# Four-block tiles for the sliding-window scores, the maxima's low part on GpSimd, packed constants and new tables of orders in a four-layer attention kernel

## The chip, the cores and the metric

The kernel runs on one core of one Trainium2 chip. The metric is the device time of one execution in microseconds (us). Engines are named as the profile names them: PE is TensorE (PEld its weight loads), DVE is VectorE, ACT is ScalarE, POOL is GpSimd, SP is SyncE, which issues the DMAs. Each engine works through its own list of instructions in order, and semaphores tie the lists together.

## The reference

Four layers, each added to its input: A, B, A, B, over 2048 positions of width 512 with 32 heads of 16. A attends to 8 keys at distances 0, 2, ... 14. B attends to the last 256 keys, its own among them. Layer A and layer B have one set of weights each, used twice.

```python
x = x + _A_ref(_layernorm(x), A_wqkv, A_wo)
x = x + _B_ref(_layernorm(x), B_wqkv, B_wo)     # and both again
# inside B
scores = jnp.einsum("bhqd,bhkd->bhqk", q, k) * (Dh ** -0.5)
mask = (idx[:, None] - idx[None, :] >= 0) & (idx[:, None] - idx[None, :] < 256)
p = _softmax(jnp.where(mask, scores, -1e9), axis=-1)
o = jnp.einsum("bhqk,bhkd->bhqd", p, v)
```

## The kernel before, in words

The positions are cut into 8 chunks of 256 queries. The unit of work is one chunk of one layer: 16 pairs, first A on chunk n, then B on chunk n (`A0`, `B0`, ... `A15`, `B15`; the second pair of layers begins at `A8`). Projections keep float32 accuracy with float16 operands: each operand is a high and a low half, and a product is three matmuls (lines 802 to 804 and 821 to 823).

**Layer B.** A chunk of 256 queries is two query blocks of 128. Each query block needs three key blocks of 128: a far one cut by a triangle (call it L), a middle one that is needed whole (F), and its own, cut by the other triangle (H). The stacked queries and keys lie in `stk`; two heads share a matmul pass, one in rows 0 to 63 and one in rows 64 to 127 of PE ("par"). Score tiles are PSUM tiles `q_sc` of 128 x 2 x 512 float32 (two banks); there are two of them for all of what follows.

- *Maxima first.* The 32 heads go in four groups `j`. For each of the 8 pairs (u, query block) in a group, PE writes a tile `sq` of two heads x three key blocks (lines 1129 and 1132), DVE merges the two triangles into one block with COPY_PREDICATED (line 1148, two heads x 128 elements) and takes the maximum with TENSOR_REDUCE (line 1150, 512 elements). In the first chunk of a layer, where L does not exist, line 1143 does both for one head at a time.
- *The maxima's way.* DVE transposes the group's 32 maxima (`mturn`, line 1158), ACT makes their high half in float16 (`mhigh`, line 1161), DVE the low half (`mlow`, line 1164, scalar_tensor_tensor on `mr` and `mt`, both in SBUF). SP writes them to DRAM (`md`, line 1169) and back into two rows of `stk` (line 1174), so that the second score pass subtracts the maximum inside the matmul.
- *Probabilities.* For each of a group's two head-quads `hq`, key chunk b (the one before, or this one) and half i, PE writes a transposed score tile `sk` of three blocks (lines 1203 and 1205), ACT takes the exponential into `p` (line 1209, 768 elements), and after two of these POOL zeroes the triangles (line 1218, 1024 elements). Then `values` (line 1235) multiplies with the values `vt` in float32: 8 matmuls, four of 256 columns and four of 128, in four column groups of PE.

**Layer A** multiplies keys and queries elementwise (`pr`, line 950, added at 957), reduces with `sel` on PE (964), spreads the softmax's weights with `selt` (1023), and weighs the values (`pw`, 1036; summed at 1041 on DVE or 1043 to 1045 on POOL).

**Weights** are prepared by `prep` at the start: squares on ACT (674), a transpose on PE (681, tiles `pam`), a scale from DVE (687 to 693), sent to all partitions by PE (696) and copied (700); then the high half on ACT (724) and the low half on DVE (726).

**What sets the order.** Every step is entered by `plan.add(engine, cost, function, reads, writes)`. The table `ORDER` gives each step its place on its engine's list, part by part (`pA`, `pB`, `W`, `A0`, `B0`, ...); a negative entry sends a step that may run on either of two engines to the other one. `Plan.order` then lays the steps of all engines out in one sequence. `W` holds `IDLE` steps of three matmuls on `selt` that only keep PE's clock up while the weights load.

Of the kernel before, what the change touches and what calls it, by code (L numbers as in the profile page):

```python
# [1386 lines left out]
```

## Time and profile before

| | |
|---|---|
| three runs | 1388.22, 1389.94, 1395.54 us (median 1389.94) |
| the profiled execution | 1386.94 us, of which the span from first to last instruction is 1385.2 us |
| mean granted PE clock | 0.988 |
| ACT | busy 736.3 us (53%) in 1075 instructions |
| DMA | 139.29 MB, 101 GB/s in the mean |
| idle steps before the work starts | 110 steps of three matmuls |

"Busy" is time in which an engine had at least one instruction under way; matmul ends are modelled, so a busy PE isn't a full PE. In a group of instructions stand the line, the engine, the operation, what it writes and reads, the shapes, the count, the busy time and the mean of one in ns. A wait is written "who line <- whom line: us in total, times, longest". A row of the timeline has its start, its duration and the merged count at the end.

### The profile page before, as it was taken

What the parts mean: (1) busy time and instruction counts of PE and PEld (TensorE: products, weight loads), DVE (VectorE), ACT (ScalarE), POOL (GpSimd) and SP (SyncE); (2) the same over time, 40 slices, a digit from 0 to 9 for tenths busy, and PEclk for the clock granted to TensorE, in tenths of its full rate; (3) what the DMA queues carried; (4) which work ended last, traced back from release to release, by engine and by line L of the source; (5) the groups of instructions that cost most, each with busy time, mean ns of one, the idle gap of its engine ahead of it and who ended that gap; (6) DMA issues with size and microseconds to landing.
All of it is one profiled execution on the core that took longest, in us unless ns stands there. A gap on an engine that the chain in (4) does not pass through costs nothing.

```text
span 1385.2 us, 34153 instructions
## 1 busy us (share of the span) xinstructions
PE 1278.8 (92%) x13546; PEld 743.3 (54%) x13546; DVE 1183.7 (85%) x2030; ACT 736.3 (53%) x1075; POOL 946.4 (68%) x963
## 2 busy tenths in 40 slices
PE   7888999999999999998899979999999999998976
PEld 6655645555555555555455545655565555543532
DVE  4898898898988898797898979988988989888674
ACT  6442535655555564564555445565655565555554
POOL 3285778786776657968576647869688877866342
PEclk9999999999999999999999999999999999999989
DMA  7425144434334452333434334444434335234312
GB/s 217 119 51 138 36 116 105 114 91 113 84 97 109 100 130 75 91 94 85 121 78 122 100 96 86 119 113 103 123 90 120 85 95 119 49 108 109 113 47 62
DMA packets 172416, 139.29 MB, mean 101 GB/s; under 512 B 105184, under 2 KB 131296, under 8 KB 172256
## 3 DMA queue, kind: packets, MB, share of 16 engines
q1 hardware_dynamic: 172000, 136.85, 37.9%
q8 instruction: 106, 1.74, 0.5%
q14 instruction: 54, 0.44, 0.1%
q10 hardware_dynamic: 256, 0.26, 0.1%
HBM read 67.11 MB, written 43.48 MB: 80 GB/s over the span
## 4 chain that ended last, share of the span: by engine, by line
PE 37%; DVE 33%; DMA 8%; issue 7%; POOL 6%; ACT 5%; SPq 4%; DVEq 0%; POOLq 0%; ACTq 0%
DVE m L1150 8%; PE av L1235 6%; DVE sq L1148 5%; PE pq L802 5%; DVE pw L1036 4%; PE pq L803 4%; PE pq L804 4%; PE sk L1203 3%; PE sq L1129 2%; ACT p L1209 2%; DVE pr L950 2%; DVE j L1143 2%; PE po L821 2%; DVE mt L1164 2%; PE po L823 2%
## 5 line engine op out<-in xcount | busy, mean ns | idle before, releaser
L1209 ACT ACTIVATE p<-sk,sclB 128x768 f32<-128x768 f32 x480 | 423.6, 900 | 274.5 <-PE sk L1205 252.6
L1218 POOL TENSOR_SCALAR_AFFINE_SELECT p<-p 128x1024 f32<-128x1024 f32 x240 | 266.1, 1117 | 171.0 <-ACT p L1209 167.3
L1150 DVE TENSOR_REDUCE m<-sq 128x2 f32<-128x512 f32 x448 | 310.4, 693 | 15.4
L1148 DVE COPY_PREDICATED sq<-maskt,sq 128x256 f32<-128x256 int16 x448 | 188.9, 422 | 77.0 <-PE sq L1132 70.2
L1235 PE MATMUL av<-p,v 128*32 128x128 f32 (+1 forms) x3840 | 200.2, 334 | 7.3 <-DVE el L1067 4.0
L950 POOL TENSOR_TENSOR pr<-kv,q 128x1024 f32<-128x1024 f32 x69 | 155.1, 2256 | 21.5 <-DVE pr L957 13.1
L1203 PE MATMUL sk<-stk,stk 64*128 64x256 f16 x960 | 130.6, 279 | 26.1 <-DVE m L1150 16.6
L1235 PEld LDWEIGHTS av<-p,v 128*32 128x32 f32 x3840 | 104.2, 110 | 94.0 <-issue 36.3
L1036 DVE TENSOR_TENSOR pw<-pb,kv 128x1024 f32<-128x1024 f32 x128 | 152.1, 1213 | 1.6 <-PE pb L1023 1.4
L1043 POOL TENSOR_TENSOR pw<-pw 128x512 f32<-128x512 f32 x92 | 117.1, 1273 | 51.6 <-DVE pw L1036 51.5
L1129 PE MATMUL sq<-stk,stk 48*128 48x128 f16 (+1 forms) x896 | 112.8, 252 | 22.6 <-DVE m L1150 13.3
L1132 PE MATMUL sq<-stk,stk 48*128 48x128 f16 (+1 forms) x1024 | 124.2, 246 | 7.9 <-DVE m L1143 5.6
L1203 PEld LDWEIGHTS <-stk 64*128 64x128 f16 x960 | 52.4, 93 | 129.1 <-issue 69.4
L1129 PEld LDWEIGHTS <-stk 48*128 48x128 f16 x896 | 48.1, 93 | 114.5 <-issue 58.1
L957 POOL TENSOR_TENSOR pr<-pr,pr 128x1024 f32<-128x1024 f32 x35 | 83.8, 2396 | 32.7 <-DVE pr L950 32.3
L1205 PE MATMUL sk<-stk,stk 64*128 64x128 f16 x960 | 104.5, 217 | 0.0
L950 DVE TENSOR_TENSOR pr<-kv,q 128x1024 f32<-128x1024 f32 x59 | 86.4, 1478 | 3.1 <-POOL pr L957 3.0
L802 PE MATMUL pq<-xh,wA1h 128*128 128x256 f16 x256 | 70.7, 276 | 3.6 <-DMA xh<-xm 3.2
L1064 ACT ACTIVATE eh<-pq 128x512 f16<-128x512 f32 x64 | 37.3, 596 | 67.7 <-PE pq L804 49.0
L803 PE MATMUL pq<-xl,wA1h 128*128 128x256 f16 x256 | 70.2, 274 | 3.1 <-DMA xl<-xn 3.1
L802 PE MATMUL pq<-xh,wB1h 128*128 128x256 f16 x256 | 70.2, 274 | 2.4 <-DVE xr L859 1.3
L1044 POOL TENSOR_TENSOR pw<-pw 128x256 f32<-128x256 f32 x92 | 67.0, 728 | 7.2
(184 smaller groups left out, 3185.3 us busy)
## 6 DMA issues: line engine op xcount, KB each, us to landing
stk<-re SPq DMA_DIRECT2D x256, 96.0 KB
re<-eh SPq DMA_DIRECT2D x128, 128.0 KB
xm<-xr SPq DMA_DIRECT2D x32, 256.0 KB
re<-el SPq DMA_DIRECT2D x64, 128.0 KB
xr<-xm SPq DMA_DIRECT2D x16, 512.0 KB
oc<-os SPq DMA_DIRECT2D x120, 64.0 KB
os<-scr SPq DMA_DIRECT2D x15, 512.0 KB
x<-in_A_x_dram SPq DMA_DIRECT2D x8, 512.0 KB
```

The costliest lines, as they stand in the source:

```text
L802: nc.tensor.matmul(ps[mp].t[:, i], wh, xh, start=k == 0, stop=False)
L803: nc.tensor.matmul(ps[mp].t[:, i], wh, xl, start=False, stop=False)
L950: E.tensor_mul(pr.t, window(kv[1].t, m, P * n, P), qb)
L1036: nc.vector.tensor_mul(pw.t, pb.t.unsqueeze(1).broadcast_to([P, 2, W, 64]), v)
L1129: nc.tensor.matmul(ps.t[:, par, 0 : (2 - qb) * P], lhs, stk[hf, bef][r, col, qb * P :], start=True, stop=True)
L1132: nc.tensor.matmul(ps.t[:, par, (2 - qb) * P : 3 * P], lhs, stk[hf, now][r, col, : (1 + qb) * P], start=True, stop=True)
L1148: nc.vector.copy_predicated(t[:, :, 0:P], maskt[:, 0:P].bitcast(I16).unsqueeze(1).broadcast_to([P, 2, P]), t[:, :, 2 * P : 3 * P])
L1150: nc.vector.tensor_reduce(out=m[:, 0:2, u, qb], in_=t[:, :, 0 : 2 * P], op=ALU.max, axis=AX.X)
L1203: nc.tensor.matmul(o[:, two], k[:, jf * P : (jf + 1) * P], q, start=True, stop=True)
L1209: nc.scalar.activation(pt.t[:, :, 2 * i : 2 * i + 2].rearrange("p s m q -> p m s q"), ps.t[:, :, : 3 * P].rearrange("p m (s q) -> p m s q" ...
L1218: nc.gpsimd.affine_select(out=v, in_=v, pattern=[[0, 8], [-1 if b == 0 else 1, P]], compare_op=ALU.is_gt if b == 0 else ALU.is_ge, fill=0. ...
L1235: nc.tensor.matmul(o, v[:, jj, 17 * h : 17 * h + 32], rhs, start=z == 0 and (b == 0 or first), stop=z == 1 and b == 1, tile_position=(0, 3 ...
```

## The change

Names of the new kernel are used with its own line numbers, which the lists below show.

1. **Maxima by kind of block.** The tiles now hold four blocks per head instead of three. A group has four tiles `st` (both triangles of both query blocks of one u: 2 heads x 4 blocks) and two tiles `sf` (the whole blocks F of two u's). Every matmul has 128 columns. `m` has two halves, one for each kind, joined by a new maximum on DVE ahead of the transpose (two operands in SBUF).
2. **Probabilities by kind of block.** For each head-quad there are three tiles of kinds F, L and H, eight matmuls of 128 columns each, an exponential of 1024 elements, a mask on POOL for L and H alone, and `values` of 8 matmuls of 128 columns. `p` has 5 buffers of 1080 elements instead of 3 of 1536.
3. **The maxima's low half** is taken on POOL, from maxima that ACT has scaled first (two ACT instructions instead of one).
4. **B's weights** are scaled in place on ACT, copied to float16 on ACT, and subtracted by a step that may run on DVE or POOL.
5. **Packed constants.** The identity lies in the third value buffer until `border(2)` overwrites it; the scales lie in two tiles; `maskt` has 256 columns instead of 384; some small tiles have one buffer instead of two.
6. **New tables.** All of `ORDER` is new, and `IDLE` is 80 instead of 110. Of the steps that may run on two engines, DVE now has 66 of the products `pr` (59 before) and 18 of the scalings `oc` (7), POOL 62 (69) and 12 (23); the others moved by one or two.

```diff
-IDLE = 110
+IDLE = 80
-                       ("pxt", 2), ("pp6", 3), ("pe2", 1), ...
+                       ("pxt", 2), ("pp6", 5), ("pe2", 1), ...
+                if T == "B":
+                    plan.add("ACT", 1.05, lambda j=j, s=s, at=at: nc.scalar.activation(at(j), at(j), AF.Copy, scale=psc[T, s][:, 1:2]),
+                             r=[*touched[j], vsc[s]], w=touched[j])
...
+                    plan.add("POOL", 2.2, lambda E, f=split: f("l", E), r=[...], w=[vwt[T, s]], mode="S", alt=("DVE", 1.13))
...
+            def block(ps, at, u, qb, back, hf=hf, hp=hp):
+                col = 4 * hp + u
+                kt, kb = (bef if qb == 0 else now, 1 - qb) if back is None else (bef if back else now, qb)
+                for par in range(2):
+                    r = slice(64 * par, 64 * par + 48)
+                    nc.tensor.matmul(ps.t[:, par, at * P : (at + 1) * P], stk[hf, 0][r, col, qb * P : (qb + 1) * P],
+                                     stk[hf, kt][r, col, kb * P : (kb + 1) * P], start=True, stop=True)
...
+                            nc.vector.copy_predicated(v[:, :, 0::2], maskt[:, 0:P]..., v[:, :, 1::2])
+                            nc.vector.tensor_reduce(out=m[:, 0, :, us[0]], in_=v[:, :, 0::2], op=ALU.max, axis=AX.X)
...
+                    nc.vector.tensor_reduce(out=o, in_=v, op=ALU.max, axis=AX.X)
...
             def mturn(m=m, mr=mr):
-                nc.vector.transpose(mr.t, m.rearrange("p a u q -> p (a u q)"))
+                a, b = (m[:, z, :, :, 1] if first else m[:, z].rearrange("p a u q -> p (a u q)") for z in range(2))
+                nc.vector.tensor_tensor(out=a, in0=a, in1=b, op=ALU.max)
+                nc.vector.transpose(mr.t, m.rearrange("p z a u q -> p (z a u q)"))
             def mhigh(mr=mr, mt=mt):
-                nc.scalar.activation(mt.t[:, 0], mr.t, AF.Copy, scale=1.0 / MC)
+                nc.scalar.activation(mr.t, mr.t, AF.Copy, scale=1.0 / MC)
+                nc.scalar.copy(mt.t[:, 0], mr.t)
             def mlow(mr=mr, mt=mt):
-                nc.vector.scalar_tensor_tensor(mt.t[:, 1], mr.t, 1.0 / MC, mt.t[:, 0], op0=ALU.mult, op1=ALU.subtract)
+                nc.gpsimd.tensor_tensor(out=mt.t[:, 1], in0=mr.t, in1=mt.t[:, 0], op=ALU.subtract)
...
-                for b in ((1,) if first else (0, 1)):
-                    for i in range(2):
+                for kind in "FH" if first else "FLH":
+                    pt = buf("pp6", [P, 4, HALO + C], F32, "p6", ...)
...
+                        nc.scalar.activation(o, i, AF.Exp, scale=scl["B", 1])
+                    if kind != "F":
...
+                                nc.tensor.matmul(acc.t[32 * mm : 32 * mm + 32, hq, qb * P : (qb + 1) * P], v[:, 17 * (H * kb + h) : ...],
+                                                 p[:, mm % 2, 2 * (mm // 2) + qb], ..., tile_position=(0, 32 * mm), skip_group_check=True)
...
+    plan.add("POOL", 0.4, lambda: border(2), w=[vidf, vborder])
```

What this and the tables make of the lists is shown at three places.

DVE, the end of group 0 of chunk 7 in the first layer B, before: `sq_7_0_u_qb` are the group's tiles, `m_123` its maxima, `pw` belongs to layer A.

```order
L1148 COPY_PREDICATED sq_7_0_2_1_9774<-maskt,sq_7_0_2_1_9774 128x2x128
L1150 TENSOR_REDUCE m_123<-sq_7_0_2_1_9774 128x2
L1148 COPY_PREDICATED sq_7_0_3_0_9788<-maskt,sq_7_0_3_0_9788 128x2x128
L1150 TENSOR_REDUCE m_123<-sq_7_0_3_0_9788 128x2
L1036 TENSOR_TENSOR pw_0_0_1_9821<-pb_0_0_1_9795,kv_0_2_9234 128x1024
L1036 TENSOR_TENSOR pw_0_0_0_9843<-pb_0_0_0_9793,kv_0_2_9234 128x1024
L1148 COPY_PREDICATED sq_7_0_0_1_9838<-maskt,sq_7_0_0_1_9838 128x2x128
L1150 TENSOR_REDUCE m_123<-sq_7_0_0_1_9838 128x2
L1148 COPY_PREDICATED sq_7_0_3_1_9863<-maskt,sq_7_0_3_1_9863 128x2x128
L1150 TENSOR_REDUCE m_123<-sq_7_0_3_1_9863 128x2
L1158 STREAM_TRANSPOSE mr_7_0_9891<-m_123 128x32
L1036 TENSOR_TENSOR pw_0_1_0_9898<-pb_0_1_0_9869,kv_0_2_9234 128x1024
```

The same place now: `st_7_0_u` are tiles of triangles, `sf_7_0_w` tiles of whole blocks, `m_118` the maxima.

```order
L1142 COPY_PREDICATED st_7_0_1_10547<-maskt,st_7_0_1_10547 128x4x128
L1143 TENSOR_REDUCE m_118<-st_7_0_1_10547 128x2x2
L1142 COPY_PREDICATED st_7_0_2_10566<-maskt,st_7_0_2_10566 128x4x128
L1143 TENSOR_REDUCE m_118<-st_7_0_2_10566 128x2x2
L1162 TENSOR_REDUCE m_118<-sf_7_0_0_10586 128x2x4
L1162 TENSOR_REDUCE m_118<-sf_7_0_1_10612 128x2x4
L1035 TENSOR_TENSOR pw_0_0_0_10634<-pb_0_0_0_10624,kv_0_2_10052 128x1024
L1142 COPY_PREDICATED st_7_0_3_10650<-maskt,st_7_0_3_10650 128x4x128
L1143 TENSOR_REDUCE m_118<-st_7_0_3_10650 128x2x2
L1035 TENSOR_TENSOR pw_0_0_1_10688<-pb_0_0_1_10626,kv_0_2_10052 128x1024
L1172 TENSOR_TENSOR m_118<-m_118 128x16
L1173 STREAM_TRANSPOSE mr_7_0_10718<-m_118 128x32
```

A group's maxima were 16 instructions over eight tiles and are now 10 over six; the joining maximum (L1172) stands ahead of the transpose, and the low half no longer follows it on DVE.

POOL at the same place, before: it sums layer A's `pw` in three steps each, and zeroes triangles of `p`.

```order
L1043 TENSOR_TENSOR pw_0_0_0_9843<-pw_0_0_0_9843 128x2x256
L1044 TENSOR_TENSOR pw_0_0_0_9843<-pw_0_0_0_9843 128x2x128
L1045 TENSOR_TENSOR o_0_9845<-pw_0_0_0_9843 128x2x64
L1218 AFFINE_SELECT p_6_6_0_9819<-p_6_6_0_9819 128x1024
L935 COPY ha_0_2_9944<-kv_0_2_9234 128x56
```

And now, with the low half (`mt`) between two such sums:

```order
L1043 TENSOR_TENSOR pw_0_0_1_10688<-pw_0_0_1_10688 128x2x128
L1044 TENSOR_TENSOR o_0_10666<-pw_0_0_1_10688 128x2x64
L1180 TENSOR_TENSOR mt_7_0_10772<-mr_7_0_10718,mt_7_0_10772 128x32
L1042 TENSOR_TENSOR pw_0_1_1_10746<-pw_0_1_1_10746 128x2x256
L1043 TENSOR_TENSOR pw_0_1_1_10746<-pw_0_1_1_10746 128x2x128
```

POOL has 64 such low halves; if the maxima are late, the sum of `pw_0_1_1` and what follows waits behind this one.

PE at the start, before: the first transpose of squares (`pam`) is the 152nd row of its list.

```order
L1347 LDWEIGHTS selt
L1347 MATMUL idle_323<-selt 128x256
L681 MATMUL pamA_327<-idf,amA_254 1x128
L1347 LDWEIGHTS selt
L1347 MATMUL idle_331<-selt 128x256
```

Now it is the 20th:

```order
L1365 LDWEIGHTS selt
L1365 MATMUL idle_192<-selt 128x256
L669 MATMUL pamA_219<-v_124,amA_209 1x128
L1365 LDWEIGHTS selt
L1365 MATMUL idle_223<-selt 128x256
```

25 idle steps (75 matmuls) stood ahead of it, now 3 (9 matmuls). Counted over PE's whole list, the form of the matmul (whole array, two row halves, four column groups) changes 1227 times before and 1003 times now, and the columns that stream through in each form are the same but for the idle steps.

More of the change, by code (lines that the diff above doesn't have):

```diff
@@ L623 @@
     wt, vwt, psc, scl, vscl = {}, {}, {}, {}, {}
+    scales = [cst.tile([P, 10], F32, name=f"scales{i}") for i in range(2)]
     for T in "AB":
         for s in range(4):
-            psc[T, s] = cst.tile([P, 2], F32, name=f"psc{T}{s}")
+            psc[T, s] = scales["AB".index(T)][:, 2 * s : 2 * s + 2]
             for z in "hl":
@@ L742, in norm @@
         rs = buf("psm", [P, 2, 2], F32, "rs", f"rs{l}_{c}")
-        b6 = buf("psm", [P, 2, 6], F32, "b6", f"b6{l}_{c}")
+        b6 = [buf("ps1", [P, 6], F32, "b6", f"b6{l}_{c}_{t}") for t in range(2)]
         vmv, vrs = [Val(mv), Val(mv)], Val(rs)
@@ new lines, in layer_b, with tri, tritop, full @@
+            vq = [vst[hf, 0, hp], vst[hf, now, hp], *([] if first else [vst[hf, bef, hp]])]
+            for w in range(2):
+                for us in ((2 * w, 2 * w + 1),) if first else ((2 * w,), (2 * w + 1,)):
+                    ps = buf("q_sc", [P, 2, 512], F32, "sc", f"st{l}_{c}_{j}_{us[0]}")
+                    vps = Val(ps)
+                    def tri(us=us, ps=ps, block=block):
+                        at = 0
+                        for u in us:
+                            for qb in range(2):
+                                for back in (False,) if first else (True, False):
+                                    block(ps, at, u, qb, back)
+                                    at += 1
+                    def tritop(us=us, ps=ps, m=m):
+                        v = ps.t.rearrange("p a (x k) -> p a x k", k=P)
+                        if first:
+                            nc.vector.tensor_tensor(out=v, in0=v, in1=maskt[:, P:].unsqueeze(1).unsqueeze(1).broadcast_to([P, 2, 4, P]), op=ALU.add)
+                            nc.vector.tensor_reduce(out=m[:, 0, :, us[0] : us[0] + 2].rearrange("p a u q -> p a (u q)"), in_=v, op=ALU.max, axis=AX.X)
+                        else:
+                            nc.vector.copy_predicated(v[:, :, 0::2], maskt[:, 0:P].bitcast(I16).unsqueeze(1).unsqueeze(1).broadcast_to([P, 2, 2, P]), v[:, :, 1::2])
+                            nc.vector.tensor_reduce(out=m[:, 0, :, us[0]], in_=v[:, :, 0::2], op=ALU.max, axis=AX.X)
+                    plan.add("PE", 0.235, tri, r=vq, w=[vps], mode="R", act=0.2)
+                    plan.add("DVE", 2.4 if first else 1.33, tritop, r=[vps], w=[vm])
+                if first and w == 0:
+                    continue
+                ps = buf("q_sc", [P, 2, 512], F32, "sc", f"sf{l}_{c}_{j}_{w}")
+                vps = Val(ps)
+                def full(w=w, ps=ps, block=block):
+                    for at in range(4):
+                        if first:
+                            block(ps, at, at, 1, None)
+                        else:
+                            block(ps, at, 2 * w + at // 2, at % 2, None)
+                def fulltop(w=w, ps=ps, m=m):
+                    v = ps.t.rearrange("p a (x k) -> p a x k", k=P)
+                    o = m[:, 1, :, :, 1] if first else m[:, 1, :, 2 * w : 2 * w + 2].rearrange("p a u q -> p a (u q)")
+                    nc.vector.tensor_reduce(out=o, in_=v, op=ALU.max, axis=AX.X)
+                plan.add("PE", 0.235, full, r=vq, w=[vps], mode="R", act=0.2)
+                plan.add("DVE", 1.2, fulltop, r=[vps], w=[vm])
@@ L1225, in values @@
-                    def values(hh=hh, hq=hq, b=b, pt=pt, jf=jf, jo=jo, qo=qo, two=two, one_=one_, acc=acc):
-                        v = vt[(c - 1 + b) % 3]
-                        for z in range(2):
-                            jj = jf if z == 0 else jo
+                                    nc.tensor.matmul(ps.t[:, par, at * P : (at + 1) * P], stk[hf, kt][r, col, kb * P : (kb + 1) * P],
+                                                     stk[hf, 0][r, col, qb * P : (qb + 1) * P], start=True, stop=True)
@@ new lines, in layer_b, with mask @@
+                    used = [now] if first else used
+                    plan.add("PE", 0.235 if len(qbs) == 2 else 0.125, scores, r=[vst[hf, 0, hp], vst[hf, "m", hp], *(vst[hf, x, hp] for x in used)],
+                             w=[vps], mode="R", act=0.2 if len(qbs) == 2 else 0.1)
+                    plan.add("ACT", 1.06 if len(qbs) == 2 else 0.6, expo, r=[vps, vscl["B", 1]], w=[vp])
+                    if kind != "F":
+                        def mask(kind=kind, view=view):
+                            v = view().rearrange("p a x k -> p (a x) k")
+                            nc.gpsimd.affine_select(out=v, in_=v, pattern=[[0, 8], [-1 if kind == "L" else 1, P]],
+                                                    compare_op=ALU.is_gt if kind == "L" else ALU.is_ge, fill=0.0, base=0,
+                                                    channel_multiplier=1 if kind == "L" else -1)
+                        v0, vp = vp, Val(pt)
+                        plan.add("POOL", 1.06, mask, r=[v0], w=[vp], mode="S")
@@ L1238, in layer_b @@
                     nxt = Val(acc)
-                    plan.add("PE", 0.67, values, r=[vp2, *vvt[(c - 1 + b) % 3], *([chain] if chain else [])], w=[vacc, nxt], mode="C", act=0.16)
+                    bs = {"F": (0, 1), "L": (0,), "H": (1,)}[kind]
+                    bs = (1,) if first else bs
+                    plan.add("PE", 0.45 if len(qbs) == 2 else 0.23, values, r=[vp, *(x for b in bs for x in vvt[(c - 1 + b) % 3]), *([chain] if chain else [])],
+                             w=[vacc, nxt], mode="C", act=0.107 if len(qbs) == 2 else 0.055)
```

173 lines of the change are left out of this document (73 added, 100 removed), and 477 rows, old and new, of the table ORDER.

## The prediction

> **What bounds the kernel now.** I read the page's busy shares first, then the windows, then the chain of work that ended last, then the waits. The page:
>
> ```profile
> span 1385.2 us, 34153 instructions
> PE 1278.8 (92%) x13546; PEld 743.3 (54%) x13546; DVE 1183.7 (85%) x2030; ACT 736.3 (53%) x1075; POOL 946.4 (68%) x963
> PE 37%; DVE 33%; DMA 8%; issue 7%; POOL 6%; ACT 5%; SPq 4%; DVEq 0%; POOLq 0%; ACTq 0%
> DVE m L1150 8%; PE av L1235 6%; DVE sq L1148 5%; PE pq L802 5%; DVE pw L1036 4%; PE pq L803 4%; PE pq L804 4%; PE sk L1203 3%; PE sq L1129 2%; ACT p L1209 2%; DVE pr L950 2%; DVE j L1143 2%; PE po L821 2%; DVE mt L1164 2%; PE po L823 2%
> ```
>
> Two windows of the steady stage (length, then busy time of PE, PEld, DVE, ACT, POOL), and three waits:
>
> ```profile
> 880.00:960.00 80.00, 78.73 (x896) 45.34 (x898) 72.52 (x116) 46.37 (x68) 63.71 (x64) 1.00 0.39 104
> 1040.00:1120.00 80.00, 77.97 (x865) 45.58 (x864) 69.77 (x110) 46.15 (x68) 64.80 (x64) 1.00 0.41 107
> DVE sq L1148 <- PE sq L1132: 70.2, 98, 3.3
> PE sk L1203 <- DVE m L1150: 16.6, 29, 1.8
> PE sq L1129 <- DVE m L1150: 13.3, 29, 1.3
> ```
>
> PE and DVE bound the steady stage together. Both are nearly full (DVE 87 to 91% of a window), the chain passes back and forth between them, and each waits for the other at the two score tiles in PSUM. ACT (53%) and POOL (68%) have room. So DVE's work counts with a weight between its rows' share of the chain and one, and the same holds for PE.
>
> **Maxima on DVE.** The old tile costs, by shape and by start times:
>
> ```profile
> L1150 DVE TENSOR_REDUCE m<-sq 128x2 f32<-128x512 f32 x448 | 310.4, 693 | 15.4
> L1148 DVE COPY_PREDICATED sq<-maskt,sq 128x256 f32<-128x256 int16 x448 | 188.9, 422 | 77.0 <-PE sq L1132 70.2 <-ACT p L1209 3.3 <-PE sq L1129 1.1
> 710.04 0.42 DVE L1148 COPY_PREDICATED sq<-maskt,sq 128x256 f32<-128x256 int16 x1
> 710.49 0.69 DVE L1150 TENSOR_REDUCE m<-sq 128x2 f32<-128x512 f32 x1
> 711.10 0.42 DVE L1148 COPY_PREDICATED sq<-maskt,sq 128x256 f32<-128x256 int16 x1
> L1036 DVE TENSOR_TENSOR pw<-pb,kv 128x1024 f32<-128x1024 f32 x128 | 152.1, 1213 | 1.6 <-PE pb L1023 1.4
> L1143 DVE CUSTOM_DVE_ANT_0 j<-sq,maskt 128x256 bf16<-128x256 f32 x64 | 27.0, 421 | 4.3 <-PE sq L1132 1.4 <-DVE m L1143 0.5
> L1143 DVE CUSTOM_DVE_ANT_0 j<-sq,maskt 128x128 bf16<-128x128 f32 x64 | 18.6, 290 | 10.4 <-PE sq L1132 7.6
> ```
>
> Copy to reduce is 0.45 us, reduce to next copy 0.61: 1.06 a tile, 8.48 a group. L1143 gains 131 ns for 128 elements, so 256 more cost some 0.26 us, 512 more 0.52. A triangle tile is then 0.45 + 0.26 + 0.61 = 1.32, a whole one 0.61 + 0.52 = 1.13 (the 1024 elements of L1036 took 1.21), a group 4 x 1.32 + 2 x 1.13 = 7.54. That is 0.94 less; with 1.21 for the whole tiles 0.78 less. I take 0.86, times 56 groups = -48 us of DVE. In the first chunks (8 groups) three larger instructions replace L1143's; nothing is taken. On the chain L1150 has 8% of 1385 = 111 us of its 310, L1148 5% = 69 of 189, so weight 0.37; at weight one it is -48. I take 0.6, because the windows leave DVE only about a tenth idle: **-29** (-18 to -48).
>
> **The low half and the joining maximum.** Lines of `mt`, and the operation that POOL holds longest:
>
> ```profile
> L1164 DVE SCALAR_TENSOR_TENSOR mt<-mr,mt x64: 156/408/2339, 134.2 to 1352.6; 128x32 f16<-128x32 f32 x64
> L1164 DVE SCALAR_TENSOR_TENSOR mt<-mr,mt 128x32 f16<-128x32 f32 x64 | 39.9, 623 | 4.7 <-ACT mt L1161 4.4
> L950 POOL TENSOR_TENSOR pr<-kv,q 128x1024 f32<-128x1024 f32 x69 | 155.1, 2256 | 21.5 <-DVE pr L957 13.1 <-ACT kv L928 7.0 <-ACT q L926 1.0
> L950 DVE TENSOR_TENSOR pr<-kv,q 128x1024 f32<-128x1024 f32 x59 | 86.4, 1478 | 3.1 <-POOL pr L957 3.0
> L1045 POOL TENSOR_TENSOR o<-pw 128x128 f32<-128x128 f32 x92 | 43.1, 469 | 7.2
> PE sk L1203 <- DMA stk<-md: 2.3, 3, 1.1
> PEld L1203 <- DMA stk<-md: 0.9, 1, 0.9
> ```
>
> 32 elements need 156 ns, and took up to 2339, about POOL's 2256: a DVE operation with two operands in SBUF stands still while POOL works on its own. Removing it gives DVE 39.9 us back. The joining maximum is again such an operation, 64 times, on 16 elements: 156 ns each if it never met POOL (10 us), 623 if it meets it as often (39.9). I take the second, since nothing in the lists keeps it away from POOL: **0** (at best -30 on DVE, -18 in time).
>
> The Trainium skill states the rule (SBUF — State Buffer, "Who interferes with whom"): a VectorE instruction with two SBUF inputs contends with a GpSimd instruction that reads SBUF, and whichever starts first holds the shared ports to its end. It speaks against the change, since what is taken from DVE comes back as another two-input instruction; the row's 156 to 2339 ns agrees, and by the rule the sum is my 0.
>
> On POOL the low half costs at most 64 x 0.469 = 30 us, covered by its idle third. Its queue is new: an instruction that waits there for ACT holds up the masks behind it, and the maxima come later by ACT's second step and by what stands ahead on POOL. PE has waited 3.2 us in all for these DMAs, so there was slack: 0.
>
> **PE.** The score matmuls are cut from 256 to 128 columns.
>
> ```profile
> 717.22 1.51 PE L1235 MATMUL av<-p,v 128*32 128x256 f32 x32
> 718.66 0.28 PE L1203 MATMUL sk<-stk,stk 64*128 64x256 f16 x2
> 718.78 0.22 PE L1205 MATMUL sk<-stk,stk 64*128 64x128 f16 x2
> 718.93 0.28 PE L802 MATMUL pq<-xh,wA0h 128*128 128x256 f16 x1
> 726.05 0.28 PE L1129 MATMUL sq<-stk,stk 48*128 48x256 f16 x2
> 726.17 0.22 PE L1132 MATMUL sq<-stk,stk 48*128 48x128 f16 x2
> 726.22 0.28 PE L1203 MATMUL sk<-stk,stk 64*128 64x256 f16 x2
> 726.34 0.22 PE L1205 MATMUL sk<-stk,stk 64*128 64x128 f16 x2
> ```
>
> By start times a pair of 256 columns takes 0.12 us and a pair of 128 takes 0.05, each with its own weights, so a tile goes from 0.17 to 4 x 0.055 = 0.22 and a group from 16 x 0.17 = 2.7 to 12 x 0.22 = 2.6. The values (1.44 us for two steps of 16 records) stream the same columns. Nothing, then, in the rate. But where the form changes (718.78 to 718.93) 0.15 passes instead of 0.05: some 0.09 lost, and the list has 224 fewer changes. 224 x 0.09 = -20 us of PE; at PE's share of the chain (37% of 1385 = 512 of 1279 busy, 0.40) -8, at weight one -20. I take **-9**. Fewer tiles also mean a quarter fewer hand-overs; PE's own waits for DVE's maxima were 16.6 + 13.3 = 30 us: **-5** (0 to -7).
>
> **Exponentials and moved steps.**
>
> ```profile
> L1209 ACT ACTIVATE p<-sk,sclB 128x768 f32<-128x768 f32 x480 | 423.6, 900 | 274.5 <-PE sk L1205 252.6 <-PE av L1235 10.1 <-POOL pw L1044 4.3
> L1309 DVE TENSOR_TENSOR oc<-oc,os 128x512 f32<-128x512 f32 x7 | 5.6, 814 | 1.7 <-DMA stk<-re 1.1 <-issue 0.6
> ```
>
> 480 exponentials become 352 of 1024 elements and 16 of 512. In proportion one takes 1.2 us (422 + 10 = 432 us); with a fixed part it is less. About even, on an engine that waited 252.6 us for PE here: 0. DVE takes over 7 products (7 x 1.478) and 11 scalings (11 x 0.814), some +19, less five steps of other kinds that went to POOL, by the same two rows 4 to 7: +14, at 0.37 **+5** (0 to +14).
>
> **The start.**
>
> ```profile
> 7.43 11.11 PE L1347 MATMUL idle<-selt 128*128 128x256 f16 x75 [7.43 <-POOL selt L619]
> 8.45 0.19 ACT L674 ACTIVATION_READ_ACCUMULATOR wA1l<-stk 128x1 f32 x1
> 24.08 2.47 DVE L726 SCALAR_TENSOR_TENSOR wA1l<-stk,pscA,wA1h 128x1024 f16<-128x1024 f32 x2
> 26.80 0.27 PE L802 MATMUL pq<-xh,wA1h 128*128 128x256 f16 x1
> 92.90 5.13 DVE L726 SCALAR_TENSOR_TENSOR wB1l<-stk,pscB,wB1h 128x512 f16<-128x512 f32 x2
> ```
>
> The squares of the first weights were ready at 8.64, but 75 idle matmuls held PE until 18.5; nine of them take 1.3 us. That could bring the first projection, at 26.80, forward by up to 9.7. The old run's next gate was `wA1l`, done at 26.5; its ACT step now waits while ACT normalises x and squares the second weights, so I take -6. B's low halves were slow on DVE (5.13 us for one half of `wB1l`); as plain subtractions some go to POOL, but ACT gets eight scalings more: -2. Together **-8** (0 to -14).
>
> **Sum.** -29 + 0 - 9 - 5 + 5 - 8 = -46 us. From the profiled execution's 1386.94 (span 1385.2 and 1.7 around it) that is 1341; the median of the three runs, 1389.94, lies 3 above the profiled one, so the forecast for a median is **1344 us**, and by the bounds of the terms some 1303 to 1377.
>
> **Rivals.**
> - *PE alone sets the pace.* It has 92% against 85%, and 97 to 98% in the windows. DVE's 48 us are then worth only idle time; left are -20 and -8: 1362. Against it: PE's ends are modelled, and DVE has 33% of the chain.
> - *The port takes it back.* DVE has 18 more two-input steps and the maximum; if each maximum meets a whole product of POOL (2.26 us) instead of 0.62, that is 64 x 1.64 = 105 us on DVE, at 0.37 +39: 1383. For it: the maximum of 2339; against: the median of 408.
> - *The port stays free for the maximum.* -18: 1326.
> - *Slower: the maxima arrive late.* PE takes its list in order, so if a `sk` tile stands at its head while the low half waits on POOL, everything on PE waits. ACT's second step is 0.2 us, half a product on POOL 1.1: 64 x 1.3 = 83 us if all of it shows, 1427. It turns the sign when more than 46 / 64 = 0.7 us a group shows. Against it: the 3.2 us of waits for `stk<-md`.
> - *Slower: short matmuls are bound by their weights.* If a pair of 128 columns can't follow a pair of 128 at 0.055 us but takes 0.10 us, near a weight load's time, when four stand in a row, a tile loses 4 x 0.04 = 0.16, 728 tiles 116 us of PE, at 0.40 to 1 +46 to +116: about 1425. At weight 0.40 it turns the sign from 0.04 a pair on. Against it: 726.17 to 726.22, though no run of four stands in this trace.
>
> The Trainium skill has a rule for that (TensorE: Matmul & The Clock Gate, "Back-to-back issue gap"): a stream of weight load and matmul pairs of 128 columns goes at about 81 ns for each matmul, not the 55 of the columns. By it eight matmuls would take 0.65 us a tile and the kernel would be far slower; the pair at 726.17 passed in 0.05 us, so the trace doesn't agree for two row halves.
>
> That the lists don't hold what the change says is out: DVE's 896 instructions for maxima beyond the first chunks are 560 in the new list.
>
> **How the numbers follow.** Forecast 0.58, PE alone 0.14, port worse 0.08, port free 0.08, late maxima 0.07, short matmuls 0.05. From no change a measurement here can tell about 0.5%, 7 us. Faster: 0.56 + 0.13 + 0.04 + 0.08 = 0.81; same: 0.02 + 0.01 + 0.03 + 0.01 = 0.07; slower: the rest, 0.12. The range 1303 to 1383 takes in the forecast's bounds, PE alone, port free and half of port worse, and leaves out some 0.16.
>
> **What would show it.** In the new profile COPY_PREDICATED of 512 near 0.69 us, the reduction of 1024 near 1.2; the joining maximum with a mean near 0.6; DVE's busy time down by some 50 to 60, PE's waits for tiles down; the first projection near 21 us; waits for `stk<-md` still a few us. Wrong would be: DVE less busy but the span the same (PE), score pairs of 128 that start over 0.08 apart, or `sk` waiting for `md`.

## The result and the profile after

The changed kernel takes 1368.6 us in the median of 4 runs (1366.8 to 1370.5), the kernel before beside it 1389.8 (1388.2 to 1395.5): a ratio of 0.984 with a 95% interval of 0.981 to 0.987. It is faster by 21 us; the forecast was 46 us faster, 1344 us in a range of 1303 to 1383. The profiled execution took 1367.4 us, with a span of 1365.6.

The page of the changed kernel, span, busy times and the chain's shares by engine:

```profile
span 1365.6 us, 40923 instructions
PE 1247.1 (91%) x17296; PEld 825.0 (60%) x17296; DVE 1149.1 (84%) x1489; ACT 732.7 (54%) x1035; POOL 945.8 (69%) x1018
PE 35%; DVE 28%; DMA 11%; POOL 10%; issue 6%; SPq 5%; ACT 5%; DVEq 0%; POOLq 0%; ACTq 0%
```

VectorE has 34.6 us less to do than before and TensorE 31.7. The chain holds less of both and more DMA (8 to 11%) and GpSimd (6 to 10%). Two windows of the steady stage, at the places shown of before, say that nothing else has become the bound there:

```profile
880.00:960.00 80.00, 77.15 (x1157) 52.26 (x1159) 72.12 (x95) 44.37 (x63) 67.14 (x71) 1.00 0.40 102
1040.00:1120.00 80.00, 78.45 (x1180) 53.39 (x1175) 71.09 (x96) 48.82 (x67) 60.35 (x68) 1.00 0.42 109
```

TensorE and VectorE are as full as before. The new instructions on VectorE, from the page's groups and, for the last row, from the list of one tile's operations (minimum, median and maximum in ns):

```profile
L1142 DVE COPY_PREDICATED st<-maskt,st 128x512 f32<-128x512 int16 x224 | 154.0, 687 | 48.5 <-PE st L1119 40.1
L1143 DVE TENSOR_REDUCE m<-st 128x4 f32<-128x512 f32 x224 | 154.9, 691 | 7.7
L1162 DVE TENSOR_REDUCE m<-sf 128x8 f32<-128x1024 f32 x120 | 145.3, 1215 | 25.3 <-PE sf L1119 24.8
L1172 DVE TENSOR_TENSOR m<-m x64: 111/264/1935, 144.4 to 1331.1; 128x16 f32<-128x16 f32 x56, 128x8 f32<-128x8 f32 x8
```

The prices are those of the prediction (0.69 and 1.2 us; the joining maximum has a mean of 0.48 where 0.62 was taken). VectorE's idle time ahead of these instructions is nearly what it was: 77.0 us before L1148, now 48.5 and 25.3 us. So the steady stage looks as forecast, and the start doesn't. Windows of the start, of the kernel before and of the changed one:

```profile
80.00:90.00 10.00, 9.31 (x65) 6.26 (x66) 8.52 (x29) 5.55 (x8) 9.17 (x9) 1.00 0.24 72
150.00:160.00 10.00, 9.21 (x96) 6.30 (x95) 7.88 (x36) 5.43 (x8) 5.57 (x8) 1.00 0.22 42
```

```profile
80.00:90.00 10.00, 0.00 (x0) 0.00 (x0) 8.73 (x13) 4.90 (x7) 0.16 (x1) 0.50 0.25 52
90.00:100.00 10.00, 8.44 (x35) 4.15 (x36) 2.12 (x4) 0.00 (x0) 5.55 (x8) 0.69 0.01 2
150.00:160.00 10.00, 3.97 (x16) 1.46 (x17) 5.84 (x5) 1.10 (x2) 5.70 (x3) 0.71 0.14 32
```

From 80 to 90 us TensorE does nothing at all, and it is granted half its clock. Who is waited for there is in the timeline and the waits of the changed kernel:

```profile
79.97 8.00 SPq L1354 DMA_DIRECT2D stk<-pad  x8
89.84 1.67 POOL L852 TENSOR_TENSOR ol<-o,oh 128x512 f16<-128x512 f32 x1 [17.58 <-DMA stk<-pad]
91.56 0.61 PE L822 MATMUL po<-wA3h,ol 128*128 128x512 f16 x1 [14.73 <-POOL ol L852]
```

```profile
POOL ol L852 <- DMA stk<-pad: 25.0, 2, 17.6
PE po L822 <- POOL ol L852: 21.9, 4, 14.7
```

GpSimd wants to make the low half of A's output (`ol`) at 72 us and stands still for 17.6 us, until transfers that read `pad` have landed; a second such wait, 7.5 us, ends at 154. `pad` holds the constant rows that stand below the keys and queries. In the changed kernel it takes turns with A's output halves in their two rotating buffers, and its transfers write over the place where B's weights are staged, so they can't start before these have been split. In the kernel before it had a buffer of its own.

To see where time is won and lost, I take from each trace the end of the fourth copy of `av` in a chunk (the evictions of B's accumulated values, L1270 before, L1287 now). The difference to the kernel before, in us, with the two main experiments beside it:

| end of | before | changed | e1_pad_own | e5_pad_early |
|---|---|---|---|---|
| chunk 0 | 204 | +15 | +4 | -1 |
| chunk 3 | 449 | +17 | +6 | -1 |
| chunk 7 | 782 | 0 | -14 | -15 |
| chunk 11 | 1093 | -3 | -18 | -19 |
| chunk 14 | 1320 | -13 | -29 | -32 |
| span | 1385.2 | -19.6 | -32.6 | -38.9 |

The changed kernel is 15 us late after its first chunk, wins 28 in the next fourteen and 6 in the last stretch.

### The profile page after: what moved, and what is told of

It is laid out like the page before. It is cut to its first block, busy times and chain, and to the rows that moved or that the text cites. A ratio compares the mean times of both kernels' runs of the same rounds, so it can differ in the third digit from the quotient of the medians.

```text
span 1365.6 us, 40923 instructions
## 1 busy us (share of the span) xinstructions
PE 1247.1 (91%) x17296; PEld 825.0 (60%) x17296; DVE 1149.1 (84%) x1489; ACT 732.7 (54%) x1035; POOL 945.8 (69%) x1018
## 4 chain that ended last, share of the span: by engine, by line
PE 35%; DVE 28%; DMA 11%; POOL 10%; issue 6%; SPq 5%; ACT 5%; DVEq 0%; POOLq 0%; ACTq 0%
PE av L1248 5%; PE pq L801 5%; DVE pw L1035 4%; PE pq L802 4%; PE pq L803 4%; DVE st L1142 4%; DVE m L1143 3%; DVE m L1162 3%; DMA stk<-re 3%; PE st L1119 2%; DVE pr L949 2%; PE po L820 2%; PE po L822 2%; PE po L821 2%; SPq L1087 1%
## 5 line engine op out<-in xcount | busy, mean ns | idle before, releaser
L1142 DVE COPY_PREDICATED st<-maskt,st 128x512 f32<-128x512 int16 x224 | 154.0, 687 | 48.5 <-PE st L1119 40.1
L1223 ACT ACTIVATE p_H<-sk_H,scales 128x1024 f32<-128x1024 f32 x128 | 142.2, 1114 | 73.6 <-PE sk_H L1213 57.2
L1234 POOL TENSOR_SCALAR_AFFINE_SELECT p_H<-p_H 128x1024 f32<-128x1024 f32 x128 | 146.8, 1151 | 43.9 <-ACT p_H L1223 43.7
L1223 ACT ACTIVATE p_F<-sk_F,scales 128x1024 f32<-128x1024 f32 (+1 forms) x128 | 135.4, 1060 | 59.9 <-PE sk_F L1213 52.5
L1162 DVE TENSOR_REDUCE m<-sf 128x8 f32<-128x1024 f32 x120 | 145.3, 1215 | 25.3 <-PE sf L1119 24.8
L1223 ACT ACTIVATE p_L<-sk_L,scales 128x1024 f32<-128x1024 f32 x112 | 124.4, 1113 | 77.0 <-PE sk_L L1213 72.9
L1143 DVE TENSOR_REDUCE m<-st 128x4 f32<-128x512 f32 x224 | 154.9, 691 | 7.7
L1234 POOL TENSOR_SCALAR_AFFINE_SELECT p_L<-p_L 128x1024 f32<-128x1024 f32 x112 | 124.7, 1117 | 34.3 <-ACT p_L L1223 34.3
L1119 PE MATMUL st<-stk,stk 48*128 48x128 f16 x1920 | 95.1, 220 | 18.0 <-DVE m L1143 6.6
L1248 PE MATMUL av<-p_H,v 128*32 128x128 f32 x2048 | 81.1, 277 | 1.7 <-POOL p_H L1234 1.6
```

Of the source, the lines that this page charges most:

```text
L1119: nc.tensor.matmul(ps.t[:, par, at * P : (at + 1) * P], stk[hf, 0][r, col, qb * P : (qb + 1) * P], stk[hf, kt][r, col, kb * P : (kb + 1) * ...
L1142: nc.vector.copy_predicated(v[:, :, 0::2], maskt[:, 0:P].bitcast(I16).unsqueeze(1).unsqueeze(1).broadcast_to([P, 2, 2, P]), v[:, :, 1::2])
L1143: nc.vector.tensor_reduce(out=m[:, 0, :, us[0]], in_=v[:, :, 0::2], op=ALU.max, axis=AX.X)
L1162: nc.vector.tensor_reduce(out=o, in_=v, op=ALU.max, axis=AX.X)
L1223: nc.scalar.activation(o, i, AF.Exp, scale=scl["B", 1])
L1234: nc.gpsimd.affine_select(out=v, in_=v, pattern=[[0, 8], [-1 if kind == "L" else 1, P]], compare_op=ALU.is_gt if kind == "L" else ALU.is_g ...
```

## The experiments

All times are medians; a time is compared with that of the experiment's own base, and the ratio goes against the kernel before, run on the same chip. With intervals of 0.003 to 0.005 to either side, two experiments can be told apart from some 5 to 7 us on.

### The start: three causes apart

**e1_pad_own.** The pad gets a buffer that nobody wants so early:

```
+    pads = buf("po4", [P, 4, C], F32, "ob", "pads")
...
-        pad = buf("poh", [16, C], F16, "o", f"pad{some[0]}")
...
+        pad = lambda k=some[0]: pads.t.rearrange("p a b -> p (a b)").bitcast(F16)[0:16, k * C : (k + 1) * C]
```

> The pad rows for the score operands get a buffer that nothing else wants at the start (B's output buffer, first used near 190 us), in place of one of the two buffers of the low and high halves of A's output. Theory: the changed kernel lost its start there, because `ol` stood still for 17.6 us at 72 and for 7.5 us at 147 until the pad's transfers had landed. Then the waits of `ol` for `pad` go, TensorE's hole from 77 to 91 us closes, and the time falls from 1368.6 by 15 to 22 us, to about 1350 (1346 to 1354, ratio to the kernel before 0.969 to 0.974). Rival: the weights of B, whose last low halves are made at 91 to 94 us and which every step of B waits for, are the gate; the hole only moves behind them, and the time stays above 1360.

1355.8 us, ratio 0.9746 (0.9718 to 0.9773): 13 us faster than the changed kernel, a little short of the 15 to 22. The wait for the pad is gone, and behind it stands another; VectorE and TensorE in this kernel:

```profile
78.36 1.20 DVE L719 TENSOR_TENSOR wB2l<-stk,wB2h 128x1024 f16<-128x1024 f32 x1
...
88.11 1.22 DVE L949 TENSOR_TENSOR pr<-kv,q 128x1024 f32<-128x1024 f32 x1
89.24 0.69 DVE L852 TENSOR_TENSOR ol<-o,oh 128x512 f16<-128x512 f32 x1
```

```profile
89.99 0.61 PE L822 MATMUL po<-wA3h,ol 128*128 128x512 f16 x1 [9.64 <-DVE ol L852]
```

The second token half of `ol` is VectorE's, and in its new order it stands behind the low halves of B's weights. (In the kernel before GpSimd made both halves, at 73 and 79 us.) The rival wasn't right that B's weights gate everything, but part of the loss does sit behind them.

**e5_pad_early.** As e1_pad_own, with five steps of VectorE moved ahead of those low halves (places 66 to 70 of its order):

```
+EARLY = {66: 57.3, 67: 57.6, 68: 57.7, 69: 61.3, 70: 61.6}
...
+        if t.eng == "DVE" and self.scope in ("A0", "B0"):
+            t.place = EARLY.get(t.place, t.place)
```

> As e1_pad_own, and on VectorE five steps of the first chunk (A's low half `ol` of the second token half, its two residual additions, the statistics for B) stand ahead of the low halves of B's weights, where the old order had them, and no longer behind them. Theory: what e1_pad_own still loses at the start against the forecast (it is 4 us late at the end of the first pair of layers where the forecast was 8 us early) stands in that queue: `ol` of the second half waits from 79.1 to 89.2 us behind five low halves and products, and TensorE waits 9.6 us for it. Then the time falls by 5 to 9 us against e1_pad_own, to about 1349 (ratio to before 0.967 to 0.971). Rival: the weights' low halves, which now come later, are what the first step of B waits for; then it falls by less than 2 us or rises.

1347.2 us, ratio 0.968 (0.964 to 0.972): 8.6 us faster than e1_pad_own, as expected. `ol` now starts at 79.31, and the window in which TensorE did nothing is full:

```profile
79.31 0.67 DVE L855 TENSOR_TENSOR ol<-o,oh 128x512 f16<-128x512 f32 x1
```

```profile
80.00:90.00 10.00, 9.40 (x68) 6.54 (x68) 9.72 (x17) 4.41 (x6) 7.47 (x10) 1.00 0.22 30
```

Part of the hole has moved: in the next window, 90 to 100 us, TensorE is busy for 5.5 us, where it was for 9.9 in e1_pad_own. This version is faster than both kernels.

**e11_early_idle.** As e5_pad_early, with the idle matmuls back at the front:

```
     "W": [
+        *[0] * 22,
         2, 11, 59, 21, 15, 1, 8, 10, 4, 18, 25, 90, 19, 128, 7, 22, 9, 84, 0, 5, 54, 50, 134, 20, 138, 133, 78, 132, 76, 102, 126, 40, 121, 135, 58,
...
-IDLE = 80
+IDLE = 102
```

> As e5_pad_early, with 66 more idle matmuls ahead of the first transposes of TensorE, so that 75 stand there as in the kernel before. It prices the cut from 75 to 9 by itself. The prediction: the first projection goes from about 21 back to 26 or 27 us and the time rises by 6. Rival: with the idle matmuls the clock is at full speed from the first projection on (in the changed kernel it was granted at 0.55 to 0.77 from 15 to 25 us), which gives back what the later start takes; the time stays within 3 us of e5_pad_early.

1362.8 us, ratio 0.981 (0.977 to 0.985): 15.6 us slower than e5_pad_early. The first projection, in this kernel:

```profile
6.63 10.48 PE L1369 MATMUL idle<-selt 128*128 128x256 f16 x75 [6.63 <-POOL selt L609]
25.74 0.27 PE L804 MATMUL pq<-xh,wA1h 128*128 128x256 f16 x1
```

It comes 5 us later, at full clock, and the rival is out: the clock gives nothing back. The cut was worth more than the 6 us forecast for it. 9 us of it are there after chunk 0, 17 after chunk 14; why the distance grows later isn't settled.

### What an engine's time is worth

**e3_pad_dve_more, e6_pad_halves, e4_pad_pe_more.** Each starts from e1_pad_own; the first two add work on VectorE, the third on TensorE. In e3_pad_dve_more a line stands ahead of each joining maximum:

```
+                nc.vector.tensor_reduce(out=spare, in_=sel.rearrange("p a h -> p (a h)").unsqueeze(1).broadcast_to([P, 8, 64]), op=ALU.max, axis=AX.X)
```

In e6_pad_halves the copy of a triangle tile (and in the same way the reduction of a whole one) is made in two halves:

```
-    nc.vector.copy_predicated(v[:, :, 0::2], maskt[:, 0:P].bitcast(I16).unsqueeze(1).unsqueeze(1).broadcast_to([P, 2, 2, P]), v[:, :, 1::2])
+    for a in range(2):
+        nc.vector.copy_predicated(v[:, a, 0::2], maskt[:, 0:P].bitcast(I16).unsqueeze(1).broadcast_to([P, 2, P]), v[:, a, 1::2])
```

In e4_pad_pe_more the matmuls of a whole tile are issued three times:

```
-                    for at in range(4):
+                    for at in (0, 1, 2, 3) * 3:
```

> As e1_pad_own, with one idle reduction of 512 elements (about 0.69 us, one input, nobody reads its output) ahead of each of the 64 joining maxima: 44 us more of VectorE. It measures what VectorE's time is worth. At the weight of 0.6 that the prediction took the time rises by 26 us against e1_pad_own, at the chain's share of 0.37 by 16, at weight one by 44. Rival, TensorE alone sets the pace: it rises by less than 8.

> As e1_pad_own, with the new tiles worked on VectorE in instructions of the old sizes: each copy of 512 elements as two of 256, each whole tile's reduction of 1024 as two of 512. TensorE's tiles, tables and waits stay those of the change. By the start times of both traces a group takes 4 x 0.157 + 2 x 0.108 = 0.85 us more of VectorE, 56 groups 47 us. Theory, VectorE's work counts about half: the time rises by 21 to 28 us against e1_pad_own (0.44 to 0.6 a us). Rival, the gain came from fewer hand-overs and from TensorE, not from shorter work on VectorE: it rises by less than 10.

> As e1_pad_own, with the matmuls of every whole score tile for the maxima issued three times (the same values again): 120 tiles with 8 more pairs of 128 columns each, at the 0.055 us a pair that the prediction read some 53 us more of TensorE. It measures what TensorE's time is worth. At the weight of 0.40 that the prediction took the time rises by 21 us against e1_pad_own. Rival, TensorE alone sets the pace: it rises by 45 to 55. If TensorE weren't on the path at all: less than 5.

The busy times in the pages of e1_pad_own, e3_pad_dve_more, e6_pad_halves and e4_pad_pe_more, in this order:

```profile
PE 1241.8 (92%) x17296; PEld 823.1 (61%) x17296; DVE 1147.6 (85%) x1489; ACT 733.0 (54%) x1035; POOL 948.1 (70%) x1018
```

```profile
PE 1245.2 (91%) x17296; PEld 822.5 (60%) x17296; DVE 1180.6 (86%) x1553; ACT 733.2 (53%) x1035; POOL 953.1 (69%) x1018
```

```profile
PE 1249.0 (91%) x17296; PEld 823.8 (60%) x17296; DVE 1191.8 (87%) x1825; ACT 734.1 (53%) x1035; POOL 948.0 (69%) x1018
```

```profile
PE 1286.5 (93%) x19216; PEld 875.5 (63%) x19216; DVE 1150.0 (83%) x1489; ACT 733.5 (53%) x1035; POOL 946.7 (69%) x1018
```

| | busy time added | time | ratio to before | us per us |
|---|---|---|---|---|
| e3_pad_dve_more | VectorE +33.0 | 1375.1, +19.3 | 0.9875 (0.984 to 0.991) | 0.58 |
| e6_pad_halves | VectorE +44.2 | 1375.1, +19.3 | 0.9871 (0.983 to 0.992) | 0.44 |
| e4_pad_pe_more | TensorE +44.7 | 1379.2, +23.4 | 0.9908 (0.988 to 0.994) | 0.52 |

(In e3 44 us were issued and 33 showed: by start times the reductions took 37.8 us, the reductions of score tiles ahead of them lost 3.6 to overlap, and the joining maxima took 3.1 us less in sum.) With about 6 us of uncertainty in each difference, a microsecond of either engine is worth about half. That excludes both extremes: TensorE alone doesn't set the pace, and VectorE alone doesn't either. e6_pad_halves loses to the old instruction sizes by themselves, with tiles, waits and tables of the change: the shorter work on VectorE is a real part of the gain, 19 us where the prediction took 29 for it (its own expectation, 21 to 28, was a little high).

### The joining maximum

**e2_pad_max** (on e1_pad_own) and **e8_all** (on e5_pad_early) replace the maximum of two inputs by a reduction with one:

```
-    nc.vector.tensor_tensor(out=a, in0=a, in1=b, op=ALU.max)
...
+    ab = m.rearrange("p z a u q -> p (a u q) z").unsqueeze(1).broadcast_to([P, 2, 16, 2])
+    nc.vector.tensor_reduce(out=f.rearrange("p (r x) -> p r x", r=2), in_=ab, op=ALU.max, axis=AX.X)
```

> As e1_pad_own, and the joining maximum of the 56 later groups is one reduction with a single input in SBUF (it writes into the low half's buffer, from which the transpose reads) in place of a maximum of two inputs. Theory of the port: that instruction, 0.48 us on average in the changed kernel and up to 1.9, falls to a constant 0.15 to 0.2 us, VectorE loses 15 to 18 us of work, and at the weight of 0.6 that the prediction gave VectorE the time falls by about 10 us against e1_pad_own (6 at the weight of 0.37). Rival, TensorE alone sets the pace: the instruction gets as short, and the time stays within 3 us of e1_pad_own. Third way: its mean stays near 0.48, so the length isn't from the shared port.

> As e5_pad_early, and with the single-input joining maximum of e2_pad_max. If both theories hold, the two gains add up: 5 to 9 us for the queue at the start and 2 to 8 for the maximum, 1340 to 1349 (ratio to before 0.962 to 0.969), the fastest of all. If the maximum gives nothing, it equals e5_pad_early.

The operation in e2_pad_max, and in e1_pad_own:

```profile
L1178 DVE TENSOR_REDUCE mt<-m x56: 159/220/225, 203.2 to 1319.7; 128x32 f32<-128x64 f32 x56
```

```profile
L1172 DVE TENSOR_TENSOR m<-m x64: 111/209/1936, 138.0 to 1318.8; 128x16 f32<-128x16 f32 x56, 128x8 f32<-128x8 f32 x8
```

The long ones are gone: it was the second input that made them long, and they had stood behind GpSimd (the last section shows it). VectorE's busy time falls by 14 us (1147.6 to 1133.4). The time doesn't follow: 1353.7 against 1355.8, and 1347.1 against 1347.2, ratios 0.9717 (0.968 to 0.975) and 0.9685 (0.965 to 0.972). At half weight 7 us were due, about as much as two runs here can tell apart; e8_all shows none. The time that VectorE no longer works it waits: its waits add up to 195.7 us in e2_pad_max against 181.2, and to 184.7 in e8_all against 175.5. The 3 us that the rival (TensorE alone) had named are met, but e3_pad_dve_more and e4_pad_pe_more rule that rival out. What holds VectorE up instead wasn't tried; the low half's buffer is taken earlier in these two.

### Late maxima

The prediction had put the low half's move at nothing, since TensorE hardly waited for these transfers. Four kernels on e1_pad_own test that. **e9_pad_low_late** issues the low half on GpSimd five times; the other three have it back on VectorE and ACT's second step gone, at three places behind the transpose: **e7_pad_low_dve** with 2.5 in the line below, **e10_pad_low_next** with 0.5, **e12_pad_low_one** with 1.5.

```
-    plan.add("POOL", 0.2, mlow, r=[vms, vmt[0]], w=[vmt[1]])
...
+    plan.add("DVE", 0.2, mlow, r=[vmr, vmt[0]], w=[vmt[1]]).place = turned + 2.5
```

> As e1_pad_own, with the low half of the maxima back on VectorE, by the old two-input instruction, two instructions behind the transpose (the median place that it had before), and ACT's second step gone. It prices the move to GpSimd by itself. VectorE's work rises by the 35 us that these 64 steps took before. Theory: at half weight the time rises by 15 to 21 us. Rival: the path through ACT's second step and GpSimd's queue had cost as much as it gave; then the time stays within 5 us of e1_pad_own, or falls.

> As e1_pad_own, with the low half on GpSimd issued five times (the same values again): each group's maxima reach the transfer queue about 1.0 us later, 64 us over 64 groups, and VectorE has no work more. It separates lateness from VectorE's work, which e7_pad_low_dve had mixed: there 35 us of work would have been worth 15 to 21, the low halves ended 104 us later in sum, and the time rose by 70. Theory: lateness of the maxima is itself on the path, at about 0.5 us a us; then the time rises by 25 to 40 us. Rival, the prediction's step that there is slack: it rises by less than 8.

> As e7_pad_low_dve, but the low half stands on VectorE directly behind its transpose, so that VectorE waits for ACT's step there (about 0.3 us a group) and the low half isn't late. VectorE gets some 20 to 35 us of work and 20 us of waiting. Theory of lateness: most of the 70 us of e7_pad_low_dve goes away, and the time stays at 5 to 25 us above e1_pad_own. Rival, the place doesn't matter and the two-input instruction on VectorE itself costs the time: it stays 50 us or more above e1_pad_own.

> As e7_pad_low_dve and e10_pad_low_next, with the low half on VectorE one instruction behind its transpose, between the two places tried. Directly behind (67 us above e1_pad_own) VectorE had waited 54 us for ACT's step; two behind (70 us above) it waited 4 us, and the low halves were late by 1.6 us each. Theory, two costs that trade: one instruction behind has some of each, VectorE waits 10 to 30 us and the low halves end about 2 us behind the transposes, and the time lies clearly under both, 30 to 55 us above e1_pad_own. Rival, the work itself on VectorE costs it wherever it stands: 60 to 75 us above.

Lateness is taken from the traces, from the end of the transpose to the end of the low half, summed over the 64 groups; VectorE's wait is the row of the waits for ACT's step.

| | time, against e1_pad_own | ratio to before | lateness, median and sum | VectorE busy | waits for ACT |
|---|---|---|---|---|---|
| e1_pad_own | 1355.8 | 0.9746 | 1.21, 121 | 1147.6 | - |
| e9_pad_low_late | 1388.3, +32.5 | 1.000 (0.998 to 1.003) | 2.62, 218 | 1161.3 | - |
| e10, directly behind | 1421.7, +66 | 1.024 (1.020 to 1.028) | 0.94, 88 | 1180.5 | 53.7 |
| e12, one behind | 1391.7, +36 | 1.003 (1.001 to 1.006) | 1.95, 134 | 1175.8 | 18.1 |
| e7, two behind | 1425.6, +70 | 1.024 (1.019 to 1.029) | 2.90, 226 | 1175.0 | 4.3 |

Rows of the waits, of e10_pad_low_next, then of e7_pad_low_dve, e9_pad_low_late and e1_pad_own:

```profile
DVE mt L1179 <- ACT mt L1176: 53.7, 64, 3.6
```

```profile
SPq L1184 <- DVE mt L1179: 213.2, 45, 11.5
PE sk_L L1211 <- DMA stk<-md: 10.0, 6, 5.0
PE sk_F L1211 <- DMA stk<-md: 8.4, 3, 5.8
```

```profile
PE av L1249 <- POOL p_L L1235: 9.8, 9, 2.3
PE av L1249 <- POOL p_H L1235: 6.4, 13, 1.0
```

```profile
SPq L1186 <- POOL mt L1180: 117.5, 37, 8.4
PE av L1248 <- POOL p_H L1234: 1.8, 5, 0.6
PE av L1248 <- POOL p_L L1234: 0.8, 2, 0.4
```

The +70 of e7_pad_low_dve fits neither of its two expectations, and the +66 of e10_pad_low_next lies outside the 5 to 25 that the theory of lateness alone gave. Two costs trade against each other. Directly behind the transpose VectorE stands still for ACT 64 times, with all its queue behind it. Two instructions later it waits no more, but the low halves are late, SyncE's queue, which carries nearly all other transfers too, stands for them 213 us instead of 118, and TensorE begins to wait: 22.0 us in all for the maxima's transfers (3.1 in e1_pad_own) and 29.8 for the others that it needs, `re`, `xh` and `xl` (14.1). The place between is clearly better than both, which the theory of two costs said and the rival (the work itself) did not. So a late maximum does cost time here, though TensorE had hardly been seen to wait for one.

What lateness costs by itself is not shown. e9_pad_low_late has 96 us more of it and 14 more of VectorE's work, and takes 32.5 us more, as its theory said; but issuing the low half five times also gave GpSimd 72 us more to do (busy 1020.1 against 948.1), which its expectation left out. By the rows above TensorE waited 16.2 us for GpSimd's masks, against 2.6, while its waits for the maxima's transfers rose from 3.1 to 9.0. A third of the lateness (32.5 of 96) is therefore an upper bound. In e7_pad_low_dve half of VectorE's 27 us explains 14 of the 70; how much of the rest is the waits for transfers isn't settled. In e10_pad_low_next half of VectorE's 33 us of work and 54 of waiting is 43 of the 66; the rest is open too. All this holds for the new tables, which came together with the low half on GpSimd, not for the old ones.

## Why the prediction was wrong, point by point

- **Bound by TensorE and VectorE together: right.** Weights of 0.6 and 0.40 were taken; both came out near one half where work was added. "PE alone", whose 1362 us lies nearer to the measured 1368.6 than the forecast, had to show VectorE's 33 and 44 us as nearly nothing and is out.
- **Maxima on VectorE, -48 us: right in VectorE's work, too high in the time.** By start times (each instruction to its end or the next one's start) 56 groups went from 473 to 427 us, 0.83 us a group where 0.86 was forecast. In the time e6_pad_halves puts the sizes at 19 us, at the low end of the 18 to 48 given, not at 29.
- **Low half and joining maximum, even on VectorE: right on VectorE** (35.5 us gone, 30.9 come, by the same count). That the move costs nothing in lateness was right in its sum and wrong in its reason: the way from the transpose to the finished low half got shorter (median 1.75 to 1.21 us, sum 148 to 122). ACT's second step added 15 us, but the step itself takes 18 less on GpSimd and waits 24 less for its turn. That maxima may come later for nothing, which the prediction read from 3.2 us of waits, is not so in the new tables (e7). The rival of late maxima named the right mechanism; here it didn't come in.
- **Moved steps, +14 on VectorE:** by the same count products, sums and scalings came to +19, the weights' low halves to -10. VectorE's busy time fell by 34.6; the text's "50 to 60" had left its own +14 out.
- **TensorE: right as far as seen.** Its busy time fell by 31.7 us, of which 10.7 are idle matmuls (48.8 to 38.1); the other 21 lie near the 20 taken, and e4 gives the weight. The rival of short matmuls is out, since tiles of eight matmuls (four pairs of row halves) follow at 0.24 us, 0.06 a pair and not 0.10, in e1_pad_own:

```profile
641.15 0.40 PE L1213 MATMUL sk_L<-stk,stk 64*128 64x128 f16 x8
641.39 0.39 PE L1119 MATMUL st<-stk,stk 48*128 48x128 f16 x8
```

The Trainium skill's 81 ns for each matmul of 128 columns (TensorE: Matmul & The Clock Gate, "Back-to-back issue gap") would make 0.65 us of these eight; the trace doesn't agree for row halves.

- **The start, -8: this is the step that failed.** It came to +15, and that is 23 of the 25 us by which the forecast was missed. What it said of the first projection happened; the changed kernel's rows:

```profile
20.94 0.37 PE L801 MATMUL pq<-xh,wA1h 128*128 128x256 f16 x1 [1.11 <-DMA xh<-xm]
23.45 0.42 PE L801 MATMUL pq<-xh,wA1h 128*128 128x256 f16 x1
24.09 0.42 PE L801 MATMUL pq<-xh,wA1h 128*128 128x256 f16 x1
...
25.37 0.28 PE L801 MATMUL pq<-xh,wA1h 128*128 128x256 f16 x1
25.71 0.27 PE L801 MATMUL pq<-xh,wA1h 128*128 128x256 f16 x1
```

It starts at 20.94 where "near 21" stood, and the cut of idle matmuls was worth more than 6 (e11). But the step followed the first chunk no further than its first matmul. Two things lay behind: the pad in a buffer that A's output needs (11 us after chunk 0 by e1, 13 in the time), and that output behind B's weights on VectorE (5 us after chunk 0 by e5, 9 in the time). The prediction gave B's weights -2, and its text doesn't mention the pad's new buffer. A further 8 us, which remain when both are mended and the idle matmuls put back (e11 is 8 us late after chunk 0), have no cause shown. They are lost early: e11 starts its first projection 1 us before the old kernel does (25.74 and 26.80) and ends the first addition of A's output 6 us after it (85.4 and 79.6).
- **All the rest** was forecast at -38 (-46 without the -8 of the start) and came to -34 (28 in the chunks, 6 at the end); with the start mended e5_pad_early has -38.9 of span in all and 1347 us beside a forecast of 1344. That the sum comes so near is in part luck: by e6 the maxima's 29 were some 19, and what made up for the difference wasn't measured. That the gain in the chunks comes unevenly (17 us of it between chunks 3 and 7) isn't explained.
- **The range:** the bounds that the terms were given add up to 1301 to 1378, and to 1283 with the low half's -18, not to 1303 to 1377.

## What to carry to other kernels

When a change gives a tile another rotating buffer, ask who needs that buffer next and what the last reader of the old content waits for: one tile of constants of 512 bytes a row held up the first output by 17.6 us, in a diff whose subject was elsewhere. Follow a start through to the first point where every engine works on the chunk's output, not only to its first instruction. Where two engines share the bound, price a microsecond of each at about half, and test that by adding work and by taking some away: here 44 us of added work cost 19, but 14 us taken off VectorE at another place gave nothing that could be measured. Don't read slack from short waits, since waits of 3 us became 22 when the maxima came later. And ask of an added step whose queue it fills: four more low halves on GpSimd made maxima late and masks too.
